# A three-stage attention and MoE kernel: the last stage's first output product taken with the inner dimension outermost, and most of w_out split while it runs

## The chip, the cores and the metric

The kernel runs on one core of a Trainium2 chip. The metric is the device time of one launch in microseconds, as a median over repeated runs; lower is better.

## The reference, cut to what matters

Three layers follow one another: a bucketed attention, a mixture of experts that sends every token to one expert, and a dense two-layer network with an ELU between its products. The change is in the last of them. N is 1536 tokens, w_in is 512 x 2048, w_out is 2048 x 512, and both come as float64 although the function casts to float32.

```python
def _moe2_ref(x, w_in, w_out):
    h = x @ w_in
    g = np.where(h > 0.0, h, 1.0 * (np.exp(np.minimum(h, 0.0)) - 1.0))
    return (g @ w_out).astype(np.float32)

def reference(...):
    x = _attn_ref(q, k, v, proj)            # to [1536, 512]
    x = _moe_ref(x=x, ...)
    return _moe2_ref(x=x, ...)
```

The float64 inputs reach the kernel as pairs of 32-bit words, so a piece of w_in or w_out has to be turned into float32 bits before use.

## The kernel before, in words

Attention, the experts and the dense layer run one after the other. Every large product is computed in float16 halves: an operand is split into a high half and a low half (what the high half leaves over), and three matmuls (high by high, high by low, low by high) go into one accumulation in PSUM.

The last stage is `moe2` (L1073). The 1536 tokens are three blocks of 512. `stage1(b)` (L1088) makes the hidden activations of block b in 16 items f of 128 hidden units. For one item TensorE (PE) issues 12 matmuls into one PSUM tile `p` (L1098 to L1100: four parts of 128 inputs, three matmuls each). ScalarE (ACT) then forms `r`, `ex` and `th` (L1103, L1105, L1107), VectorE (DVE) forms `m` in two instructions (L1109, L1110), GpSimd (POOL) rounds `m` to the high half `gh` (L1111) and, for blocks 0 and 1, subtracts it to get the low half `gl` (L1113); for block 2 DVE does that subtraction (L1119). `ex` and `th` have one buffer each, so `ex` of the next item waits for L1109 of this one; `r` and `m` have two. The PSUM tag `mp` has 8 tiles, taken in turn, so PE can be up to eight items ahead of L1110, which is the last reader of `p`.

`stage2(b)` (L1124) is the second product of block b: for each of four token tiles t of 128 tokens, 16 x 3 matmuls over f (L1132 to L1134) into one PSUM tile, then one ACT copy to `o` (L1136, two buffers) and one indirect DMA issued by POOL that scatters the 128 rows to the output (L1137). The calls stand in the order stage1(0), stage1(1), stage2(0), stage1(2), stage2(1), stage2(2) (L1139 to L1146).

w_out is split by the `Feeder` (L552). It is 16 pieces of 128 x 512, piece c belonging to hidden part f = c; pieces 0 to 7 go to the tiles `wbh` and `wbl`, pieces 8 to 15 to `wah` and `wal`. One call of `step` (L601) advances a pipeline of three: it writes the low half of the oldest piece (L610, on DVE here), then the high half of the next one (L614, on ACT here), and then starts a new piece, which for float64 is three bit operations on DVE (L589, L590, L591); it then loads another piece by DMA from SyncE's queue (SP, L574) into one of 6 staging tiles. So 16 pieces take 18 steps. The tuple `M2F` (L55) says after which items f of which block a step is made: after every second item of block 0 and after every item of block 1.

The queues of each engine run in the order in which the code emits instructions. There is no other order than that of the calls above.

Of the kernel before, what the change touches and what calls it, by code (L numbers as in the profile page):

```python
# [10 lines left out]
F32 = mybir.dt.float32  # L11
I32 = mybir.dt.int32
AF = mybir.ActivationFunctionType
# [38 lines left out]
UO = 6  # L52
XN = (0, 1, 2, 2, 2, 2, 2, 5)
NWI = 0
M2F = (range(0, 16, 2), range(16), ())  # L55
LAST = 94
STG = 6
MORE = 1
# [493 lines left out]
class Feeder:  # L552
# [4 lines left out]

    def __init__(self, nc, g, depth):
        self.nc, self.g, self.depth = nc, g, depth
        self.todo, self.loaded, self.stage = [], [], [None, None]  # L560
        self.eager, self.n32, self.n, self.more, self.done, self.modes = False, 0, 0, None, {}, []

    def add(self, items):
# [37 lines left out]
    def step(self, keep=0):  # L601
        nc = self.nc
        p2, p1 = self.stage
        if p2:
            x, hi, lo, scale, mode, n = p2
            self.done[n] = self.done.get(n, 0) + 1
            if mode[1] == "p":
                nc.gpsimd.tensor_tensor(lo, x, hi, op=ALU.subtract)
            else:
                nc.vector.scalar_tensor_tensor(lo, x, scale, hi, op0=ALU.mult, op1=ALU.subtract)  # L610
        if p1:
            x, hi, lo, scale, mode, n = p1
            if mode[0] == "a":
                nc.scalar.activation(hi, x, AF.Copy, scale=scale)  # L614
            else:
                nc.gpsimd.tensor_scalar(hi, x, scale, 1.0, op0=ALU.mult, op1=ALU.mult)
        self.stage = [p1, self.first() if self.loaded and len(self.loaded) + len(self.todo) > keep else None]
        if self.eager:
            self.load()
# [20 lines left out]
WIS, WOS, GS = 2.0 ** 7, 2.0 ** 8, 2.0 ** 12  # L640
# [58 lines left out]


def routing(tc, g, pool, T, xgs, step):

    nc = tc.nc
# [32 lines left out]
    g.xg = {}  # L736
    xgs()
    step()
    nc.vector.tensor_reduce(g.sm, g.ex, axis=AX.X, op=ALU.add)
    nc.vector.tensor_scalar(g.sm, g.sm, 1e-9, None, op0=ALU.add)  # L740
# [118 lines left out]
def expert_up(nc, pool, ps, wh, wl, xh, xl, step):  # L859

    hh = pool.tile([128, 8, NW], F16, tag="hh", bufs=2, name="hh")
    hl = pool.tile([128, 8, NW], F16, tag="hl", bufs=2, name="hl")
    for f in range(8):
        p = ps.tile([128, NW], F32, tag="mp", bufs=8, name="hp")
        fs = slice(f * 128, (f + 1) * 128)
        for kk in range(4):
            w = slice(kk * 1024 + f * 128, kk * 1024 + (f + 1) * 128)
            nc.tensor.matmul(p, lhsT=wh[:, w], rhs=xh[:, kk], start=(kk == 0), stop=False)
            nc.tensor.matmul(p, lhsT=wl[:, w], rhs=xh[:, kk], start=False, stop=False)
        for kk in range(4):  # L870
            w = slice(kk * 1024 + f * 128, kk * 1024 + (f + 1) * 128)
            nc.tensor.matmul(p, lhsT=wh[:, w], rhs=xl[:, kk], start=False, stop=(kk == 3))
        nc.scalar.activation(hh[:, f], p, AF.Relu)
        nc.vector.scalar_tensor_tensor(hl[:, f], p, 0.0, hh[:, f], op0=ALU.max, op1=ALU.subtract)
        step(f)
    return hh, hl
# [196 lines left out]
def moe2(tc, es, g, w_out, out, fd):  # L1073
    nc = tc.nc
    pool = es.enter_context(tc.tile_pool(name="m2", bufs=1, reuse_waits="tile"))
    ps = es.enter_context(tc.tile_pool(name="m2ps", bufs=1, reuse_waits="tile", space=PSUM))
    parts = g.wb, g.wa
    g.phase = 2 * E
    fd.depth, fd.n = STG, 0
    fd.add(g.wo)  # L1080
    fd.load()
    fd.mode64 = M2
    s1 = 1.0 / (YS * WIS)
    G = {}
    lngs = pool.tile([128, 1], F32, name="lngs")
    nc.vector.memset(lngs, math.log(GS))

    def stage1(b):  # L1088
        gh = pool.tile([128, 16, 512], F16, tag="gh", bufs=2, name="gh")
        gl = pool.tile([128, 16, 512], F16, tag="gl", bufs=2, name="gl")  # L1090
        G[b] = gh, gl
        cols = slice(b * 512, (b + 1) * 512)
        late = None
        for f in range(16):
            p = ps.tile([128, 512], F32, tag="mp", bufs=8, name="p1")
            fs = slice(f * 128, (f + 1) * 128)
            for kk in range(4):
                nc.tensor.matmul(p, lhsT=g.wih[:, kk, fs], rhs=g.yh[:, kk, cols], start=(kk == 0), stop=False)  # L1098
                nc.tensor.matmul(p, lhsT=g.wih[:, kk, fs], rhs=g.yl[:, kk, cols], start=False, stop=False)  # L1099
                nc.tensor.matmul(p, lhsT=g.wil[:, kk, fs], rhs=g.yh[:, kk, cols], start=False, stop=(kk == 3))  # L1100

            r = pool.tile([128, 512], F32, tag="r", bufs=2, name="r")
            nc.scalar.activation(r, p, AF.Relu, scale=-s1)  # L1103
            ex = pool.tile([128, 512], F32, tag="ex", bufs=1, name="ex")
            nc.scalar.activation(ex, r, AF.Exp, scale=-1.0, bias=lngs)  # L1105
            th = pool.tile([128, 512], F32, tag="th", bufs=1, name="th")
            nc.scalar.activation(th, r, AF.Tanh, scale=-0.5)  # L1107
            m = pool.tile([128, 512], F32, tag="m", bufs=MB, name="m")
            nc.vector.scalar_tensor_tensor(m, ex, GS, th, op0=ALU.add, op1=ALU.mult)  # L1109
            nc.vector.scalar_tensor_tensor(m, p, s1 * GS, m, op0=ALU.mult, op1=ALU.max)  # L1110
            nc.gpsimd.tensor_scalar(gh[:, f], m, 1.0, 1.0, op0=ALU.mult, op1=ALU.mult)  # L1111
            if b < GLP:
                nc.gpsimd.tensor_tensor(gl[:, f], m, gh[:, f], op=ALU.subtract)  # L1113
            if late:
                late()

            def late(f=f, m=m):
                if b >= GLP:
                    nc.vector.tensor_sub(gl[:, f], m, gh[:, f])  # L1119
            if f in M2F[b]:  # L1120
                fd.step()
        late()

    def stage2(b):  # L1124
        gh, gl = G.pop(b)
        for t in range(4):
            j = 4 * b + t
            p = ps.tile([128, 512], F32, tag="mp", bufs=8, name="p2")
            ts_ = slice(t * 128, (t + 1) * 128)
            for f in range(16):  # L1130
                (wh, wl), o = parts[f // 8], (f % 8) * 512
                nc.tensor.matmul(p, lhsT=gh[:, f, ts_], rhs=wh[:, o:o + 512], start=(f == 0), stop=False)  # L1132
                nc.tensor.matmul(p, lhsT=gh[:, f, ts_], rhs=wl[:, o:o + 512], start=False, stop=False)  # L1133
                nc.tensor.matmul(p, lhsT=gl[:, f, ts_], rhs=wh[:, o:o + 512], start=False, stop=(f == 15))  # L1134
            o = pool.tile([128, 512], F32, tag="o", bufs=2, name="o")
            nc.scalar.activation(o, p, AF.Copy, scale=1.0 / (GS * WOS))  # L1136
            nc.gpsimd.indirect_dma_start(out=out, out_offset=bass.IndirectOffsetOnAxis(ap=g.idx[:, j:j + 1], axis=0), in_=o, in_offset=None)  # L1137

    stage1(0)  # L1139
    stage1(1)  # L1140
    while fd.left():
        fd.step()
    stage2(0)
    stage1(2)
    stage2(1)
    stage2(2)  # L1146


def body(tc, q, k, v, proj, w_gate, w1, w2, w_in, w_out, out, dbg=None):
# [8 lines left out]
    with ExitStack() as es:  # L1158
# [12 lines left out]
        with tc.manual_schedule():  # L1171
# [40 lines left out]
            with ExitStack() as es3:  # L1212
                moe2(tc, es3, g, w_out, out, fd)
# [27 lines left out]
```

## Time and profile before

| what | value |
|---|---|
| median of 3 runs (lowest to highest) | 705.37 us (702.53 to 707.24) |
| the profiled execution | 704.08 us |
| its span in the trace | 702.0 us |
| PE busy over the span | 646.1 us (92%) |
| DVE, ACT, POOL busy over the span | 490.2, 364.2, 268.6 us |
| first matmul of the last stage | 425.42 us from the span's start |

Times in the rows below are microseconds from the start of the span, unless marked ns. The busy time of PE counts overlapping matmuls once; a matmul of 512 columns has a record of 0.38 us although the next one starts sooner, so the distance of starts is what one costs. "idle before <-X" is how long the engine stood still before an instruction and what released it.

### The profile page before, as it was taken

The numbers are of one execution on the slowest core, as the hardware profiler recorded it, in microseconds if no ns is written. First come the engines' busy times: TensorE is split into PE (matmuls) and PEld (weight loads), VectorE is DVE, ScalarE is ACT, GpSimd is POOL, SyncE is SP. The second block draws the span as 40 slices with busy tenths as digits, with TensorE's granted clock in tenths as the row PEclk, the third lists the DMA queues.
The fourth block names the chain that finished last, engine by engine and source line by source line (L and its number), as shares of the span: only waits on it lengthen the run. The fifth ranks groups of instructions, "written<-read, shape, count | busy, mean of one in ns | idle before, by whom it ended". The sixth has DMA issues, their size and how long they took to land. (4 is left out here: it accounts for less than half of the span.)

```text
span 702.0 us, 12276 instructions
## 1 busy us (share of the span) xinstructions
PE 646.1 (92%) x4584; PEld 423.1 (60%) x4584; DVE 490.2 (70%) x971; ACT 364.2 (52%) x663; POOL 268.6 (38%) x327
## 2 busy tenths in 40 slices
PE   6889999999999878899999998999688999999996
PEld 3456666666666537799999994444233444444442
DVE  6878999888867276799999996888997007710000
ACT  4567676676677425666666544455447027710000
POOL 5958788667733035000000002666347313311001
PEclk9889999999999988899999999999989999999999
DMA  5878999997852049988887835121100000000000
GB/s 174 171 143 183 210 253 232 219 199 177 160 122 57 23 123 204 276 285 294 296 286 261 292 131 211 61 90 61 60 0 1 31 30 1 0 16 31 15 31 30
DMA packets 135071, 95.49 MB, mean 136 GB/s; under 512 B 104800, under 2 KB 117088, under 8 KB 135008
## 3 DMA queue, kind: packets, MB, share of 16 engines
q1 hardware_dynamic: 133088, 88.38, 47.7%
q0 software_dynamic: 1920, 6.29, 3.0%
q8 instruction: 37, 0.61, 0.4%
q14 instruction: 26, 0.21, 0.1%
HBM read 62.93 MB, written 6.29 MB: 99 GB/s over the span
## 5 line engine op out<-in xcount | busy, mean ns | idle before, releaser
L1111 POOL TENSOR_SCALAR gh<-m 128x512 f16<-128x512 f32 x48 | 41.8, 870 | 227.5 <-DVE f L589 156.1
L339 ACT ACTIVATE A<-sp,nm 128x768 f32<-128x768 f32 x96 | 94.9, 991 | 37.9 <-DVE nm L332 32.2
L321 DVE TENSOR_REDUCE nm<-sp 128x1 f32<-128x768 f32 x96 | 91.1, 949 | 25.2 <-PE sp L317 23.2
L1098 PE MATMUL p<-yh,wih 128*128 128x512 f16 x192 | 74.8, 390 | 14.4 <-DVE m L1110 11.7
L380 ACT ACTIVATE AT<-ptA 128x512 f32<-128x512 f32 (+1 forms) x102 | 59.0, 580 | 38.1 <-PE ptA L378 31.3
L390 PE MATMUL ot<-AT,vraw 128*64 128x384 f32 x192 | 74.2, 507 | 1.8 <-ACT AT L380 1.8
L1099 PE MATMUL p<-yl,wih 128*128 128x512 f16 x192 | 74.9, 390 | 0.0
L1100 PE MATMUL p<-yh,wil 128*128 128x512 f16 x192 | 74.6, 389 | 0.0
L378 PE MATMUL ptA<-id,A 128*128 128x128 f32 x396 | 61.7, 280 | 12.3 <-ACT AT L380 10.6
L1109 DVE SCALAR_TENSOR_TENSOR m<-ex,th 128x512 f32<-128x512 f32 x48 | 34.3, 715 | 55.0 <-ACT th L1107 49.1
L316 PE MATMUL sp<-KA,QA 128*128 128x384 f16 x192 | 64.1, 334 | 3.0 <-ACT A L339 2.7
L378 PEld LDWEIGHTS ptA<-id,A 128*128 128x128 f32 x396 | 46.3, 141 | 33.0 <-ACT AT L380 27.7
L317 PE MATMUL sp<-KB,QB 76*128 76x384 f16 x192 | 63.6, 331 | 0.0
L1136 ACT ACTIVATE o<-p 128x512 f32<-128x512 f32 x12 | 7.1, 595 | 103.6 <-PE p L1134 103.6
L349 POOL TENSOR_TENSOR hl<-A,hl 128x768 f16<-128x768 f32 x30 | 49.3, 1644 | 2.5
L1105 ACT ACTIVATE ex<-r,lngs 128x512 f32<-128x512 f32 x48 | 34.7, 722 | 28.7 <-DVE m L1109 27.6
L1137 POOL DMA_INDIRECT out_dram<-o,idx x12 | 11.9, 988 | 95.1 <-ACT o L1136 95.0
L395 PE MATMUL ot<-ATD,VH 128*64 128x256 f16 x270 | 46.0, 280 | 0.0
L1113 POOL TENSOR_TENSOR gl<-m,gh 128x512 f16<-128x512 f32 x32 | 44.0, 1376 | 2.7
L1099 PEld LDWEIGHTS <-wih 128*128 128x128 f16 x192 | 19.2, 100 | 36.7 <-issue 16.1
L399 PE MATMUL ot<-AT,vraw 128*64 128x128 f32 (+1 forms) x192 | 40.0, 291 | 0.0
L360 POOL TENSOR_SCALAR hl<-A 128x768 f16<-128x768 f32 x30 | 25.3, 843 | 38.2 <-ACT A L339 38.2
(250 smaller groups left out, 1660.3 us busy)
## 6 DMA issues: line engine op xcount, KB each, us to landing
stg<-in_moe_w_dram SPq DMA_DIRECT2D x64, 512.0 KB, 5.0
stg<-in_moe_w_in_dram SPq DMA_DIRECT2D x16, 512.0 KB, 5.0
stg<-in_moe_w_out_dram SPq DMA_DIRECT2D x16, 512.0 KB, 3.2
vraw<-in_v_dram SPq DMA_DIRECT2D x8, 384.0 KB, 3.6
xd<-xr SPq DMA_DIRECT2D x16, 192.0 KB, 2.4
qraw<-in_q_dram SPq DMA_DIRECT2D x7, 384.0 KB, 4.0
kraw<-in_k_dram SPq DMA_DIRECT2D x7, 384.0 KB, 4.1
ATD<-hl SPq DMA_TRANSPOSE x30, 3.5
```

Source lines behind the costliest of these rows:

```text
L316: nc.tensor.matmul(sp[:, j, 0:384], lhsT=QA[P, h][:, c * 128:(c + 1) * 128], rhs=KA[P, h][:, kk], start=True, stop=False)
L317: nc.tensor.matmul(sp[:, j, 0:384], lhsT=QB[P, h][0:76, c * 128:(c + 1) * 128], rhs=KB[P, h][0:76, kk], start=False, stop=True)
L321: nc.vector.tensor_reduce(nm[:, 0:1], sp[:, :, 0:384], axis=AX.XY, op=ALU.max, negate=True)
L339: nc.scalar.activation(a, sp[:, :, 0:384], AF.Exp, bias=nm[:, 2:3], scale=nm[:, 1:2], accum_out=SUM[u][:, r:r + 1])
L349: LATE.append((lambda: nc.gpsimd.tensor_tensor(hl[:, 1], a, hl[:, 0], op=ALU.subtract), u, r, hl, a))
L378: nc.tensor.transpose(pt[:, cols], src[:, kt * 128:(kt + 1) * 128], g.id32)
L380: nc.scalar.activation(at[:, 0:n], pt[:, 0:n], AF.Copy)
L390: nc.tensor.matmul(ot[64:128], lhsT=vt[P][:, 1, kt, :], rhs=at, start=(kt == 0), stop=(kt == 5))
L395: nc.tensor.matmul(ot[0:64, 0:n].rearrange("p (a b) -> p a b", b=128), lhsT=VH[P][:, vs, kt, :], rhs=ATD[u][:, :, as_, kt], start=(kt == 0 ...
L1098: nc.tensor.matmul(p, lhsT=g.wih[:, kk, fs], rhs=g.yh[:, kk, cols], start=(kk == 0), stop=False)
L1099: nc.tensor.matmul(p, lhsT=g.wih[:, kk, fs], rhs=g.yl[:, kk, cols], start=False, stop=False)
L1100: nc.tensor.matmul(p, lhsT=g.wil[:, kk, fs], rhs=g.yh[:, kk, cols], start=False, stop=(kk == 3))
```

## The change

`M2F` now asks for four steps in block 0 and four in block 1, after the items 2, 6, 10 and 14 of each. The loop that made the remaining steps ahead of the second product is gone. The first block's second product is a new function, `stage2_first`: its outer loop goes over f and its inner one over the four token tiles, with four PSUM tiles open together. Ahead of the matmuls of f it emits steps until f + 3 pieces are complete in emission order (the new counter `out`, reset at the start of the calls). All four tiles are stored after the last f. The other two blocks keep the order with t outside; their loop body moved to `part2` and `store` unchanged. The diff in full:

```diff
--- before.py
+++ after.py
@@ -52,7 +52,7 @@
 UO = 6
 XN = (0, 1, 2, 2, 2, 2, 2, 5)
 NWI = 0
-M2F = (range(0, 16, 2), range(16), ())
+M2F = (2, 6, 10, 14), (2, 6, 10, 14), ()
 LAST = 94
 STG = 6
 MORE = 1
@@ -557,7 +557,7 @@
 
     def __init__(self, nc, g, depth):
         self.nc, self.g, self.depth = nc, g, depth
-        self.todo, self.loaded, self.stage = [], [], [None, None]
+        self.todo, self.loaded, self.stage, self.out = [], [], [None, None], 0
         self.eager, self.n32, self.n, self.more, self.done, self.modes = False, 0, 0, None, {}, []
 
     def add(self, items):
@@ -604,6 +604,7 @@
         if p2:
             x, hi, lo, scale, mode, n = p2
             self.done[n] = self.done.get(n, 0) + 1
+            self.out += 1
             if mode[1] == "p":
                 nc.gpsimd.tensor_tensor(lo, x, hi, op=ALU.subtract)
             else:
@@ -1121,26 +1122,42 @@
                 fd.step()
         late()
 
+    def part2(gh, gl, p, t, f):
+        ts_ = slice(t * 128, (t + 1) * 128)
+        (wh, wl), o = parts[f // 8], (f % 8) * 512
+        nc.tensor.matmul(p, lhsT=gh[:, f, ts_], rhs=wh[:, o:o + 512], start=(f == 0), stop=False)
+        nc.tensor.matmul(p, lhsT=gh[:, f, ts_], rhs=wl[:, o:o + 512], start=False, stop=False)
+        nc.tensor.matmul(p, lhsT=gl[:, f, ts_], rhs=wh[:, o:o + 512], start=False, stop=(f == 15))
+
+    def store(p, j):
+        o = pool.tile([128, 512], F32, tag="o", bufs=2, name="o")
+        nc.scalar.activation(o, p, AF.Copy, scale=1.0 / (GS * WOS))
+        nc.gpsimd.indirect_dma_start(out=out, out_offset=bass.IndirectOffsetOnAxis(ap=g.idx[:, j:j + 1], axis=0), in_=o, in_offset=None)
+
+    def stage2_first(b):
+
+        gh, gl = G.pop(b)
+        ps4 = [ps.tile([128, 512], F32, tag="mp", bufs=8, name="p2") for _ in range(4)]
+        for f in range(16):
+            while fd.out < min(16, f + 3):
+                fd.step()
+            for t in range(4):
+                part2(gh, gl, ps4[t], t, f)
+        for t in range(4):
+            store(ps4[t], 4 * b + t)
+
     def stage2(b):
         gh, gl = G.pop(b)
         for t in range(4):
-            j = 4 * b + t
             p = ps.tile([128, 512], F32, tag="mp", bufs=8, name="p2")
-            ts_ = slice(t * 128, (t + 1) * 128)
             for f in range(16):
-                (wh, wl), o = parts[f // 8], (f % 8) * 512
-                nc.tensor.matmul(p, lhsT=gh[:, f, ts_], rhs=wh[:, o:o + 512], start=(f == 0), stop=False)
-                nc.tensor.matmul(p, lhsT=gh[:, f, ts_], rhs=wl[:, o:o + 512], start=False, stop=False)
-                nc.tensor.matmul(p, lhsT=gl[:, f, ts_], rhs=wh[:, o:o + 512], start=False, stop=(f == 15))
-            o = pool.tile([128, 512], F32, tag="o", bufs=2, name="o")
-            nc.scalar.activation(o, p, AF.Copy, scale=1.0 / (GS * WOS))
-            nc.gpsimd.indirect_dma_start(out=out, out_offset=bass.IndirectOffsetOnAxis(ap=g.idx[:, j:j + 1], axis=0), in_=o, in_offset=None)
-
+                part2(gh, gl, p, t, f)
+            store(p, 4 * b + t)
+
+    fd.out = 16 - fd.left()
     stage1(0)
     stage1(1)
-    while fd.left():
-        fd.step()
-    stage2(0)
+    stage2_first(0)
     stage1(2)
     stage2(1)
     stage2(2)
```

## Rows read from the trace of the kernel before

**Rows 1.** The page's busy tenths of PE over the span, 40 slices

```profile
PE   6889999999999878899999998999688999999996
```

**Rows 2.** Last stage by stretches: busy us (x instructions) per engine, PEclk, DMA

```profile
425.40:486.60 61.20, 59.73 (x277) 27.02 (x277) 50.20 (x63) 32.73 (x58) 33.45 (x30) 1.00 0.32 114
486.60:528.80 42.20, 29.63 (x109) 11.67 (x109) 40.40 (x51) 20.71 (x37) 19.87 (x19) 0.88 0.10 35
528.80:540.84 12.04, 12.04 (x48) 5.13 (x49) 9.02 (x12) 8.79 (x16) 10.26 (x10) 0.86 0.00 1
540.84:571.92 31.08, 31.08 (x145) 14.07 (x144) 2.95 (x5) 4.18 (x8) 9.35 (x10) 1.00 0.07 26
```

**Rows 3.** Waits from 425 on (total us, times, longest), and the first in time

```profile
PE p L1098 <- DVE m L1110: 11.7, 8, 2.2
PE p L1132 <- DVE m L1110: 2.3, 1, 2.3
...
486.60 0.38 PE L1098 MATMUL p<-yh,wih 128*128 128x512 f16 x1 [1.45 <-DVE m L1110]
```

**Rows 4.** Timeline of PE, last stage: start us, us, engine, line, operation

```profile
425.42 0.38 PE L1098 MATMUL p<-yh,wih 128*128 128x512 f16 x1 [2.67 <-DVEq L1043]
...
530.12 0.63 PE L1134 MATMUL p<-wbh,gl 128*128 128x512 f16 x1
530.55 0.63 PE L1132 MATMUL p<-wbh,gh 128*128 128x512 f16 x1
...
540.84 0.38 PE L1132 MATMUL p<-wbh,gh 128*128 128x512 f16 x1
...
571.92 0.38 PE L1098 MATMUL p<-yh,wih 128*128 128x512 f16 x1
```

**Rows 5.** Timeline of DVE in block 0 of the last stage

```profile
430.11 0.69 DVE L1109 SCALAR_TENSOR_TENSOR m<-ex,th 128x512 f32<-128x512 f32 x1 [4.44 <-ACT th L1107]
...
434.49 0.68 DVE L1109 SCALAR_TENSOR_TENSOR m<-ex,th 128x512 f32<-128x512 f32 x1
...
443.22 0.69 DVE L1109 SCALAR_TENSOR_TENSOR m<-ex,th 128x512 f32<-128x512 f32 x1 [0.71 <-POOL gh L1111]
...
444.56 0.92 DVE L610 SCALAR_TENSOR_TENSOR wbl<-f,wbh 128x512 f16<-128x512 f32 x1
...
446.27 1.52 DVE L590 SCALAR_TENSOR_TENSOR f<-stg,f 128x512 int32<-128x512 int32 x1
...
448.44 0.68 DVE L1109 SCALAR_TENSOR_TENSOR m<-ex,th 128x512 f32<-128x512 f32 x1
...
450.56 0.69 DVE L1109 SCALAR_TENSOR_TENSOR m<-ex,th 128x512 f32<-128x512 f32 x1 [0.71 <-POOL gh L1111]
```

**Rows 6.** Timeline of DVE just before the last stage, w_in's pieces

```profile
420.69 0.68 DVE L610 SCALAR_TENSOR_TENSOR wil<-f,wih 128x512 f16<-128x512 f32 x1
...
421.87 0.69 DVE L590 SCALAR_TENSOR_TENSOR f<-stg,f 128x512 int32<-128x512 int32 x1
...
423.20 0.38 DVE L893 SCALAR_TENSOR_TENSOR yl<-yp,yh 128x224 f32 x1
```

**Rows 7.** Timeline of ACT in block 0, the high half of piece 1

```profile
443.03 0.61 ACT L614 ACTIVATE wbh<-f 128x512 f16<-128x512 f32 x1
```

**Rows 8.** Timeline of PE in the attention: scores, L317 then L316 changes the bank

```profile
202.33 0.33 PE L317 MATMUL sp<-KB,QB 76*128 76x384 f16 x1
202.49 0.33 PE L316 MATMUL sp<-KA,QA 128*128 128x384 f16 x1
202.66 0.33 PE L317 MATMUL sp<-KB,QB 76*128 76x384 f16 x1
```

**Rows 9.** Output stores: ACT, then POOL, then the DMA's time to landing

```profile
551.40 0.60 ACT L1136 ACTIVATE o<-p 128x512 f32<-128x512 f32 x1 [7.16 <-PE p L1134]
...
552.28 0.98 POOL L1137 DMA_INDIRECT out_dram<-o,idx  x1 [3.64 <-ACT o L1136]
...
DMA to landing us min/median/max: 2.7/2.7/2.8
```

## The prediction

> **What bounds the kernel now.** Read the page's slices first: in the last stage, which begins near slice 24, PE is full but for a dip between slices 27 and 30 [rows 1]. The page says "PE-bound with a hole". To see the hole, cut the last stage into stretches: from 425.4 to 486.6 and from 540.8 on PE is busy nearly throughout at a granted clock of 1.00; from 486.6 to 528.8 it is busy 29.6 of 42.2 us, at 0.88, while DVE is busy 40.4; and from 528.8 to 540.8 it is busy but at 0.86 [rows 2]. Then ask who was waited for: PE stood still 8 times for L1110 in the first product, 11.7 us, and once, 2.3 us, at the start of the second, first at 486.60 [rows 3]. L1110 is DVE's last read of a PSUM tile. So for the first 61 us PE runs ahead on eight PSUM tiles, and then it moves at DVE's pace, whose time goes to the split of w_out beside `m`.
>
> The timeline of PE says what the hole costs. In the undisturbed stretch 144 matmuls start between 540.84 and 571.92, 0.2158 us each (2.4 GHz). At 530.12 two starts lie 0.43 apart: the lower level, 1.2 GHz [rows 4]. Clock and waits go together: the granted clock is below 1 only in the stretch with the waits and just behind it [rows 2, 3]. Block 0's and block 1's first products and block 0's second one are 576 matmuls, 124.3 us at 0.2158; they took 571.92 - 425.42 = 146.5 [rows 4]. The excess is **22.2 us**: 14.0 of waits [rows 3], and 8.2 of low clock (39 matmuls at 0.21 extra).
>
> **The change, part by part.** Work is neither added nor removed: the same 48 bit operations, 16 high and 16 low halves, 576 matmuls, four stores. What changes is when DVE does the pieces.
>
> *Steps in the first products.* Instead of steps after 8 items of block 0 and after each of the first ten of block 1 (by then all 18 are made) there are 4 and 4. The price of a step in the chain of `m` is read from DVE in block 0: from one L1109 to the next it is 2.12 us without a step (448.44 to 450.56) and 5.22 with a full one (443.22 to 448.44); the first two steps have no low half to write and cost 4.38 (430.11 to 434.49) [rows 5]. PE needs 12 x 0.2158 = 2.59 per item. So a stepped item puts the chain 5.22 - 2.59 = 2.63 behind (1.79 for the first two) and each of the three others gives back 0.47: +1.22 per four items. With no lag at item 2, it is 1.79 at item 3, 0.38 at 6, 2.17 at 7, 0.76 at 10, 3.39 at 11, 1.98 at 14, 4.61 at 15, then in block 1 (items 16 to 31) 5.83 at 19, 7.05 at 23, 8.27 at 27 and 9.49 at 31, the last.
>
> The base of that lag: item 0's last matmul ends at 425.42 + 2.59 + 0.16 = 428.17, its L1109 starts at 430.11, 1.94 later, and both parts of `m` take 1.34 (443.22 to 444.56) [rows 4, 5]. An item n is then done on DVE at 428.86 + 2.59 (n + 1) + lag. PE may start item n once n - 8 is done, so it waits only with a lag over 8 x 2.59 - 2.59 - 3.44 = 14.7. The largest is 9.49: **PE doesn't wait in either first product**, and ends them at 425.42 + 32 x 2.59 = 508.3 instead of 528.8.
>
> *PSUM tiles of the second product.* The four tiles opened together are those that items 24 to 27 held. Item 27 is done at 428.86 + 72.52 + 8.27 = 509.65; PE wants that tile after three groups of 3 matmuls, at 510.25. Just enough; bounds 0 and 1 us, I take 0.
>
> *The pieces that are left.* Six are complete in emission order when the second product begins. DVE goes on with them without waiting for PE, since they read staging tiles only. Item 31 is done at 428.86 + 82.88 + 9.49 = 521.2, the low half of piece 6 at 521.9; PE reaches f = 6 at 508.3 + 6 x 2.59 = 523.8, so 1.9 to spare. A piece costs DVE 2.51 where POOL is idle (420.69 to 423.20, L590 0.69 in it) [rows 6] and 3.88 where POOL works (444.56 to 448.44, L590 1.52) [rows 5]. After item 31 POOL has only its last `gh` and `gl` to do, so I take 3.88 for piece 7 and 2.51 for the other eight: 0.5 to spare at f = 7, and because 2.51 is under 2.59 it doesn't shrink afterwards. Piece 15 ends at 521.9 + 3.88 + 8 x 2.51 = 545.9 against 547.2. The margin is small: 0.2 us more in each cycle of four items makes 1.4 us of lag at the end and about 0.9 of wait. Bounds: 0, and 10.3 if all nine pieces cost 3.88 (521.9 + 34.9 = 556.8 for piece 15, plus 0.7 for lag). I take 0.7, nearest the rows without POOL. ACT's high halves (0.61 each) [rows 7] have an engine to themselves there.
>
> *Does a matmul wait for more than its own piece?* It would, if writes to `wbh` were ordered against every read of it. In the step that writes the low half of piece 0 at 444.56 (it reads `wbh`) the high half of piece 1 (it writes another slice of `wbh`, and is emitted later) ran at 443.03, ahead of it [rows 5, 7]. So waits go by slices, and I cost this at 0.
>
> *f outside.* Each f is 4 x 3 matmuls, and the PSUM bank changes after three of them, 64 times in all against 4. In the attention's scores the bank changes every two matmuls: L317 to L316 across the bank 0.16, L316 to L317 within it 0.17, for 384 columns [rows 8]. Cost 0. By the Trainium skill ("TensorE: Matmul & The Clock Gate", section "A second HAM failure mode: psum-queue depth-cycling") a kernel that cycled through PSUM banks left small idle gaps between its groups and its clock swung between the two levels; that speaks against this loop, and by it the third rival below would come true.
>
> *Stores.* All four come at the end of `stage2_first`, and stand in ACT's queue ahead of stage1(2)'s first `r`. With two `o` buffers the third copy waits for the first DMA: from ACT's start 0.9 to POOL's issue and 2.7 to landing [rows 9]. First copy 1.8 us ahead of PE's end (nine matmuls), third at +1.8, fourth 1 us later (POOL's 0.98 spacing), ACT free at +3.4, when item 0 of block 2 is ready at +2.6. Late by 0.8, which eight PSUM tiles cover; without that cover it would cost those 0.8. Nothing later moves: stage1(2) and the two other second products are the same 576 matmuls at full pace.
>
> *SP's queue.* Loads follow the steps; each is issued when its staging tile is free, at least four steps before its use. Cost 0.
>
> **Sum.** The second product ends 22.2 - 0.7 = 21.5 us earlier. On the profiled execution's own time, 704.08, that is 682.6; on the median, 705.37, 683.9. I predict **683.3**, between the two, with its own range 680 to 686.
>
> **Rivals.**
>
> 1. *The late pieces pace the second product.* POOL's work, or a longer cycle in block 1, keeps DVE behind PE from f = 6 on. For: margins of 0.5 us. Against: POOL has no work left there. Price: 10.3 us at the upper bound, 692.2 on 704.08; with low clock in the proportion of before (8.2 to 14.0) 6.0 more, 698.2. A typical case is 692.
>
> 2. *The first products don't come free.* If a cycle without step beside low clocks or busier POOL were near 2.6, the lag would go on growing past 14.7, and PE would wait as it does now: about 704, no change. Against: eight pairs in block 0 repeat 7.34 us (443.22 to 450.56) [rows 5].
>
> 3. *Slower: the second product at the low clock.* If the change of bank after every three matmuls left gaps and the clock stayed at 1.2 GHz, all 192 matmuls would take 0.43 instead of 0.2158 [rows 4]: +40.6 us, 704.08 - 22.2 + 40.6 = 722.5. It decides from 105 of the 192 on (22.2 / 0.211). Against: rows 8.
>
> **How the numbers follow.** Forecast 0.80, rival 1 0.13, rival 2 0.04, rival 3 0.03. About 1% (7 us) is what a measurement of this kernel can tell from no change. Forecast and rival 1 are faster by more: 0.93; same 0.04; slower 0.03. The range goes from the lowest run less the whole 22.2 (702.53 - 22.2 = 680.3, so 680) to 691, which takes in part of rival 1.
>
> **What would show it.** PE without a wait from 425 to the end of the last matmul, at clock 1.00; the first matmul of the second product at 508.3, stage1(2)'s first at about 550; stepped items of L1109 some 5.2 apart and unstepped ones 2.1; item 31's L1110 done near 521; L590 at 0.69 from the second late piece on. Wrong if PE waits for L610 in the second product by more than 3 us, if its starts there lie more than 0.22 apart, or if it still waits for L1110 before 508.

## The result, and the profile after

The changed kernel takes 684.77 us (median of four, 680.84 to 687.91) against 703.95 for the kernel before (702.17 to 707.24): 0.9714 of its time, with a 95% interval of 0.9678 to 0.975. Timed again later beside it, it gave 682.96 against 702.39, ratio 0.9718 (0.9671 to 0.9765). One of the eleven runs of the kernel before in that second comparison was in a slower state (709.24 us): the ratio leaves it out, and the median of the other ten is 701.98. The forecast was 683.3 in a range of 680 to 691. The profiled execution took 682.41 us, its span 680.3.

The page's busy tenths of PE after the change, and its granted clock, in 40 slices:

```profile
PE   6899998999999876799999998999999999999996
PEclk9989999999999997999999999999999999999998
```

The dip of [rows 1] between slices 27 and 30 is gone. Stretches of the last stage after the change, columns as in [rows 2]:

```profile
425.40:486.60 61.20, 61.20 (x280) 27.48 (x279) 45.36 (x58) 38.15 (x66) 40.67 (x38) 0.98 0.22 81
486.60:508.00 21.40, 21.40 (x101) 9.66 (x99) 16.71 (x22) 14.40 (x26) 17.20 (x16) 1.00 0.14 48
508.00:550.00 42.00, 41.32 (x192) 18.57 (x190) 33.83 (x49) 13.79 (x23) 11.18 (x11) 1.00 0.15 51
```

PE is busy throughout both first products, and all but 0.7 us of the second one, at a granted clock of 1.00 but for 0.98 in the first of these stretches. DVE, busy for 40.4 of 42.2 us in the hole before, now has 33.8 us of work in the 42 us of the second product and makes PE wait twice there, 0.8 us together (one of the two is too short to have a mark below: at 510.10 PE starts 0.3 us late).

PE's starts, after the change, where one thing gives way to the next (L1099 is the first product, L1128 to L1130 the second):

```profile
423.30 0.38 PE L1099 MATMUL p<-yh,wih 128*128 128x512 f16 x1 [2.95 <-DVEq L1044]
...
424.40 0.63 PE L1101 MATMUL p<-yh,wil 128*128 128x512 f16 x1
424.83 0.63 PE L1099 MATMUL p<-yh,wih 128*128 128x512 f16 x1
...
507.86 0.38 PE L1128 MATMUL p<-wbh,gh 128*128 128x512 f16 x1
...
509.59 0.38 PE L1130 MATMUL p<-wbh,gl 128*128 128x512 f16 x1
510.10 0.38 PE L1128 MATMUL p<-wbh,gh 128*128 128x512 f16 x1
...
527.21 0.38 PE L1129 MATMUL p<-wbl,gh 128*128 128x512 f16 x1 [0.54 <-DVE wbl L611]
...
550.30 0.38 PE L1099 MATMUL p<-yh,wih 128*128 128x512 f16 x1
```

From the first matmul of the stage to block 2's first, "the stretch" from here on, it is 550.30 - 423.30 = 127.0 us against 146.5 [rows 4]: 19.5 less. The rest of the 21.7 us between the two profiled executions lies outside the change: the stage began 2.1 us earlier, and behind the stretch there are 130.0 us against 130.1. That start is not the change's doing: in the eleven profiled executions of this study it lies anywhere from 423.1 to 429.7.

### The profile page after: what moved, and what is told of

Same layout as the page of the kernel before. It is cut to its first block, busy times and chain, and to the rows that moved or that the text cites. A ratio compares the mean times of both kernels' runs of the same rounds, so it can differ in the third digit from the quotient of the medians.

```text
span 680.3 us, 12275 instructions
## 1 busy us (share of the span) xinstructions
PE 636.7 (94%) x4584; PEld 420.5 (62%) x4584; DVE 486.7 (72%) x971; ACT 362.8 (53%) x663; POOL 269.6 (40%) x327
## 5 line engine op out<-in xcount | busy, mean ns | idle before, releaser
L1112 POOL TENSOR_SCALAR gh<-m 128x512 f16<-128x512 f32 x48 | 39.0, 812 | 199.6 <-DMA stg<-in_moe_w_out_dram 157.4
L321 DVE TENSOR_REDUCE nm<-sp 128x1 f32<-128x768 f32 x96 | 91.0, 948 | 22.3 <-PE sp L317 20.6
L1099 PE MATMUL p<-yh,wih 128*128 128x512 f16 x192 | 73.5, 383 | 3.0 <-DVEq L1044 3.0
L1100 PE MATMUL p<-yl,wih 128*128 128x512 f16 x192 | 73.4, 382 | 0.0
L316 PE MATMUL sp<-KA,QA 128*128 128x384 f16 x192 | 63.6, 331 | 3.3 <-ACT A L339 3.0
L1110 DVE SCALAR_TENSOR_TENSOR m<-ex,th 128x512 f32<-128x512 f32 x48 | 37.7, 786 | 39.2 <-ACT th L1108 30.5
L317 PE MATMUL sp<-KB,QB 76*128 76x384 f16 x192 | 63.2, 329 | 0.0
L1114 POOL TENSOR_TENSOR gl<-m,gh 128x512 f16<-128x512 f32 x32 | 46.0, 1439 | 2.7
L1129 PE MATMUL p<-wbl,gh 128*128 128x512 f16 x96 | 36.4, 379 | 0.5 <-DVE wbl L611 0.5
```

What stands on the lines that cost most here:

```text
L316: nc.tensor.matmul(sp[:, j, 0:384], lhsT=QA[P, h][:, c * 128:(c + 1) * 128], rhs=KA[P, h][:, kk], start=True, stop=False)
L317: nc.tensor.matmul(sp[:, j, 0:384], lhsT=QB[P, h][0:76, c * 128:(c + 1) * 128], rhs=KB[P, h][0:76, kk], start=False, stop=True)
L321: nc.vector.tensor_reduce(nm[:, 0:1], sp[:, :, 0:384], axis=AX.XY, op=ALU.max, negate=True)
```

## The experiments

All are made from the changed kernel. "The stretch" is read from PE's starts in each trace.

**f outside alone.** The old steps, so that no piece is left for the second product.

```diff
-M2F = (2, 6, 10, 14), (2, 6, 10, 14), ()
+M2F = (range(0, 16, 2), range(16), ())
```

> The changed kernel with the old M2F (steps after every second item of block 0 and every item of block 1), so that f is outside but no piece is left for the second product. Theory A (the gain comes from where DVE's steps stand, and f outside is only what lets the late ones in): nothing is gained. PE waits in the first products as before, 11.7 us, and the second product then needs the PSUM tiles of items 24 to 27 within its first f instead of one after another, so that it waits for four L1110s, some 2 us each, instead of one of 2.3: the stretch from the last stage's first matmul to block 2's first is 150 to 153 us against 146.5, the kernel 3 to 7 us slower than before. Theory B (f outside helps by itself): the stretch is shorter than 146.5. Theory C (changing the bank after three matmuls costs): starts lie more than 0.2158 us apart in the second product; at 0.16 for each of 64 changes that is 10 us more than A says.

Measured: 711.36 against 704.98 us, ratio 1.0085 (1.0052 to 1.0119). The stretch is 153.9 us. PE's waits where the second product begins:

```profile
532.58 0.38 PE L1128 MATMUL p<-wbh,gh 128*128 128x512 f16 x1 [2.31 <-DVE m L1111]
536.07 0.59 PE L1128 MATMUL p<-wbh,gh 128*128 128x512 f16 x1 [2.68 <-DVE m L1111]
538.40 0.59 PE L1128 MATMUL p<-wbh,gh 128*128 128x512 f16 x1 [0.90 <-DVE m L1111]
540.54 0.59 PE L1128 MATMUL p<-wbh,gh 128*128 128x512 f16 x1 [0.70 <-DVE m L1111]
```

The four tiles are taken one after another at DVE's pace, as theory A says: 6.6 us instead of 2.3 [rows 3]. Theory B falls: the loop order by itself makes the kernel slower. So does theory C: the stretch is 0.9 us over A's upper bound, not 10, and its starts leave nothing for the change of bank. Of the 29.6 us above 576 x 0.2158, 18.3 are waits and 8.8 are starts about 0.43 apart (1.6 of that at the start of the stage). The other 2.5 are the ends of the matmuls ahead of the waits, whose records reach past the time at which the next one would have started.

**The spread of steps alone.** The second product has t outside, and the ten late steps stand ahead of it.

```diff
-    stage2_first(0)
+    while fd.left():
+        fd.step()
+    stage2(0)
```

> The changed kernel with its four and four steps, but with the second product of block 0 as before: t outside, and the ten steps left emitted ahead of it. Theory A: the first products end early (the second one starts near 84 us after the stage's first matmul, as in the changed kernel), but the first token tile needs all 16 pieces within 10.4 us, while DVE brings the last one only some 121 us after the stage's first matmul; PE waits for L610's low halves about 26 us in the first token tile, and the stretch is 151 to 155 us: 4 to 8 us slower than before. Theory B (relief of DVE in the first products carries the gain, the order of the second product is of no account): the stretch stays within 3 us of the changed kernel's 127.0.

Measured: 713.11 against 704.98 us, ratio 1.0094 (1.0059 to 1.0129); the stretch is 154.4 us, and the second product starts 82.9 us after the stage's first matmul. Who PE waited for, in total us, times and longest:

```profile
PE p L1129 <- DVE wbl L611: 13.0, 3, 7.3
PE p L1129 <- DVE wal L611: 7.6, 7, 1.1
```

The first products come free just as in the changed kernel, and everything gained is lost again in the first token tile. The waits are 20.6 us where about 26 were expected; up to the last of them, at 548.02, the first token tile is 27 us behind, and the difference is in starts further apart than 0.2158 us. So each half of the change costs about 1% by itself, and the two together gain 2.9%.

**Ten early steps instead of eight.**

```diff
-M2F = (2, 6, 10, 14), (2, 6, 10, 14), ()
+M2F = (1, 4, 7, 10, 13), (1, 4, 7, 10, 13), ()
```

> The changed kernel with ten steps in the two first products (after the items 1, 4, 7, 10, 13 of each) instead of eight. Theory A (the lag of DVE behind PE decides): three items cost 5.22 + 2 x 2.13 = 9.48 us against PE's 7.77, so the lag comes to about 15 us at item 31; the first products still run without a wait (it needs about 14.7 at item 23), but the tile of item 27, stepped before, comes some 5 us late: PE waits about 5 us in the first f of the second product and the stretch is 129.6 us plus what low clock adds (up to 2.5), 2.5 to 6 us over the changed kernel. Theory B (what counts is DVE's total work, which is the same): within 1 us of the changed kernel.

Measured: 694.62 against 704.98 us, ratio 0.9839 (0.9804 to 0.9873); the stretch is 135.5 us, 8.5 over the changed kernel's, more than the 2.5 to 6 expected. PE's waits in the stretch:

```profile
513.52 0.38 PE L1128 MATMUL p<-wbh,gh 128*128 128x512 f16 x1 [1.09 <-DVE m L1111]
515.66 0.59 PE L1128 MATMUL p<-wbh,gh 128*128 128x512 f16 x1 [1.33 <-DVE m L1111]
520.86 0.59 PE L1128 MATMUL p<-wbh,gh 128*128 128x512 f16 x1 [3.76 <-DVE m L1111]
```

The place is theory A's (no wait in the first products, then the tiles that DVE has not yet read), the size 6.2 instead of 5: three waits, one each for the tiles of items 25, 26 and 27. Low clock added more than I allowed: the second product's stretch shows a granted clock of 0.90 and takes 51.2 us, 3.6 over 41.4 + 6.2, of which 2.8 are starts 0.43 apart; another 1.4 us of such starts stand at the start of the stage. Theory B (only DVE's total counts) falls.

**No early step.**

```diff
-M2F = (2, 6, 10, 14), (2, 6, 10, 14), ()
+M2F = (), (), ()
```

> The changed kernel with no step in the two first products, so that all 18 stand in the second one, where POOL is idle and a piece costs DVE 2.51 instead of 3.88 us. Theory A: the lag at item 31 is gone, DVE is free some 86 us after the stage's first matmul, but piece 0 is complete only some 9 us after PE wants it, and the pieces then keep pace (2.51 against 2.59): one wait of about 9 us at f = 0 and 133.5 us for the stretch, 6 to 10 us over the changed kernel. Theory D (the gain comes from moving pieces to where POOL leaves DVE alone, the more the better): the time is that of the changed kernel or below it.

Measured: 696.06 against 704.98 us, ratio 0.9873 (0.982 to 0.9926); the stretch is 137.8 us. PE's waits in it, then the stretches of the first and of the second product:

```profile
517.12 0.58 PE L1128 MATMUL p<-wbh,gh 128*128 128x512 f16 x1 [7.84 <-ACT wbh L615]
518.85 0.59 PE L1129 MATMUL p<-wbl,gh 128*128 128x512 f16 x1 [1.15 <-DVE wbl L611]
```

```profile
424.60:517.10 92.50, 84.68 (x384) 37.94 (x385) 56.66 (x70) 59.44 (x97) 65.54 (x64) 0.96 0.09 35
517.10:562.40 45.30, 44.14 (x193) 19.40 (x193) 36.13 (x60) 10.63 (x17) 0.84 (x1) 0.93 0.34 117
```

Two waits for piece 0, its high half and then its low half, together of the expected size (9.0 against 9), after which the pieces keep pace for all 16 f; the rest of what it costs is mostly low clock, 1.6 us at the start of the stage and most of the 2.7 behind the waits (0.93). Theory D falls: pieces are cheaper late, but too many late ones make PE wait.

**Six early steps.**

```diff
-M2F = (2, 6, 10, 14), (2, 6, 10, 14), ()
+M2F = (4, 9, 14), (4, 9, 14), ()
```

> The changed kernel with six steps in the first products (after the items 4, 9, 14 of each) instead of eight. Theory A: a step taken out of the first products takes about 2.6 us off the lag and puts one late piece of 2.5 us in, needed 2.6 us earlier, so that PE's waits stay near 0 to 1 us: the same as the changed kernel within 1 us, with the wait for the tile of item 27 gone. Theory D (the more late the better, or every late piece makes PE wait): a difference of over 2 us to one side or the other.

Measured: 681.97 against 706.36 us, ratio 0.9639 (0.9573 to 0.9705). No wait of PE in the stretch, which takes 124.4 us, 0.1 more than 576 x 0.2158. Its two parts:

```profile
423.10:505.90 82.80, 82.80 (x384) 37.54 (x385) 58.83 (x77) 54.72 (x94) 59.34 (x57) 1.00 0.20 70
505.90:547.50 41.60, 41.60 (x195) 18.81 (x193) 34.40 (x52) 12.21 (x21) 9.19 (x9) 1.00 0.19 64
```

With this order of work nothing more than that 0.1 us is left to gain in the stretch. This one and the changed kernel were then timed side by side.

> The changed kernel unaltered, beside the one with six steps on the same chip, to tell the two apart. Theory A: two short waits in the second product (0.3 for the tile of item 27, 0.7 for the low half of piece 7), 125.4 us for the stretch where no low clock falls into it; 19 to 22 us faster than before.

> The kernel with six early steps, again. Theory A: no wait, 124.4 us for the stretch, so 1.0 us faster than the changed kernel, 0.15%, which may not show in the whole time. If it is faster by more than 2 us, the two short waits cost more than their length, by low clock for one thing.

Measured against the same 702.39 us: the changed kernel 682.96, ratio 0.9718 (0.9671 to 0.9765), six steps 682.49, ratio 0.9698 (0.9649 to 0.9747). The whole times do not tell them apart. In the traces they differ as expected: from the second product's first matmul to block 2's first it is 42.55 us with eight steps and 41.50 with six. Both executions have low clock at the start of the stage, 1.3 and 1.7 us, so that the whole stretches are 126.7 and 126.1. The two waits of the changed kernel were there again:

```profile
PE p L1129 <- DVE wbl L611: 0.5, 1, 0.5
PE p L1128 <- DVE m L1111: 0.3, 1, 0.3
```

**Four stores at once.** Two kernels take all three second products with f outside, so that the last four stores have nothing behind them; the second one gives the last two copies other buffers.

```diff
-    stage2(1)
-    stage2(2)
+    stage2_first(1)
+    stage2_first(2)
```

> The changed kernel with f outside in the second products of blocks 1 and 2 as well, so that the four stores of block 2 stand at the end of the kernel, with nothing to cover them. Cost of the loop order by itself: if changing the bank is free, the last matmul comes as many us after block 2's first as in the changed kernel. Cost of four stores at once: by theory S (each indirect DMA to the output waits for the one before to land, as the 3.48 to 3.61 us between POOL's four issues in the changed kernel suggest) the last POOL issue comes 3 x 3.5 us after the first, which is 1.9 us earlier than a last tile's store would be: about 8.5 us more than the changed kernel. By the prediction's own step (only the two o buffers tie the third copy to the first DMA, POOL's issues are 1 us apart) it is about 2.6 us more.

```diff
-        o = pool.tile([128, 512], F32, tag="o", bufs=2, name="o")
+        o = pool.tile([128, 512], F32, tag="o" if j < 10 else "m", bufs=2, name="o")
```

> The same with f outside in all three blocks, but the last two stores of block 2 use the buffers of m (free by then), so that no copy of block 2 waits for a buffer. Theory S (the DMAs wait for each other): POOL's four last issues stay some 3.5 us apart and the time is that of the kernel with two buffers, within 1 us. Theory of the two buffers: the four issues lie 1 us apart and the end comes 1.6 to 6 us earlier than with two buffers.

Measured, one run each: 691.47 and 690.84 us. From block 2's first matmul to the last it is 675.09 - 550.98 = 124.1 us with f outside everywhere and 674.40 - 550.30 = 124.1 in the changed kernel: the loop order costs PE nothing. From the last matmul to the end of the span it is 689.5 - 675.1 = 14.4 us against 680.3 - 674.4 = 5.9: 8.5 more, theory S's number. POOL's last issues with two buffers:

```profile
674.48 0.97 POOL L1135 DMA_INDIRECT out_dram<-o,idx  x1 [29.64 <-ACT o L1134]
677.96 0.97 POOL L1135 DMA_INDIRECT out_dram<-o,idx  x1 [2.51 <-ACT o L1134]
681.43 0.97 POOL L1135 DMA_INDIRECT out_dram<-o,idx  x1 [2.51 <-ACT o L1134]
684.92 0.97 POOL L1135 DMA_INDIRECT out_dram<-o,idx  x1 [2.52 <-DMA out_dram<-o,idx]
```

And with four, ACT's copies ahead of them:

```profile
672.86 2.49 ACT L1134 ACTIVATE o<-p 128x512 f32<-128x512 f32 x4 [33.29 <-PE p L1130]
...
680.69 0.97 POOL L1135 DMA_INDIRECT out_dram<-o,idx  x1 [2.51 <-DMA out_dram<-o,idx]
684.18 0.97 POOL L1135 DMA_INDIRECT out_dram<-o,idx  x1 [2.52 <-DMA out_dram<-o,idx]
```

With the four copies done in 2.49 us the issues stay 3.48 us apart and now name the DMA before as what released them. The buffers were not the tie; each write to the output waits for the one before it to land. That is not so for every indirect DMA from POOL's queue. Ahead of the changed kernel's experts POOL issues 12 that gather rows (L761), which take 4.4 to 7.2 us to land; three of them:

```profile
261.10 0.95 POOL L761 DMA_INDIRECT wih<-xd,idx  x1 [0.30 <-DVE wih L773]
262.35 0.95 POOL L761 DMA_INDIRECT wih<-xd,idx  x1 [0.30 <-issue]
263.60 0.94 POOL L761 DMA_INDIRECT wih<-xd,idx  x1 [0.30 <-issue]
```

These start 1.25 us apart. So the queue alone doesn't tie the stores to each other. That all of them write one output is the likely reason, but whether the wait is the program's or the chip's, and whether it can be left out, was not tested.

## Why the prediction was right, step by step

**The bound and the sum.** The excess of 22.2 us was there to be had: with six steps the stretch is 124.4 us, 22.1 under the 146.5 of before. The changed kernel took 19.5 of it in its profiled execution, against 21.5 forecast, and the three others with the same code in the stretch took 125.4, 125.4 and 126.7 (19.8 to 21.1). By medians the gain is 19.2 and 19.0 us (the second against 701.98). So the mechanism holds and the size is about a tenth too high: the term mis-sized is the allowance of 0.7 us for waits, which came to 1.0 (125.4 less 124.4), beside a spell of low clock at the start of the stage, for which I allowed nothing: from 424.40 on eight starts lie 0.43 apart, 1.7 us. Such a spell of 1.3 to 1.7 us is in six of the study's eleven traces; the kernel with six steps shows it in one execution and not in the other, so it doesn't come from the steps. PE stands still for 2.65 to 2.95 us just ahead of the stage in all eleven; why the spell follows in only six is not shown. That the profiled execution came within 0.2 us of my 682.6 is in part luck: its stage began 2.1 us earlier.

One reading in the prediction was off without changing the sum. The 8.2 us that it puts down to low clock are 6.5 in 32 starts at about 0.43, and 1.5 in the nine matmuls ahead of the waits: a wait counts from the end of the 0.38 us record, 0.16 after the next one would have started. The 22.2 us stand, and so does what a wait costs beyond its length, as rival 1 prices it; only not all of that is clock.

**Steps in the first products.** L1110 (L1109 before) across one full step and three items without, after the change:

```profile
456.92 0.70 DVE L1110 SCALAR_TENSOR_TENSOR m<-ex,th 128x512 f32<-128x512 f32 x1 [0.71 <-ACT th L1108]
...
462.14 0.69 DVE L1110 SCALAR_TENSOR_TENSOR m<-ex,th 128x512 f32<-128x512 f32 x1
...
464.27 0.69 DVE L1110 SCALAR_TENSOR_TENSOR m<-ex,th 128x512 f32<-128x512 f32 x1 [0.71 <-POOL gh L1112]
...
466.40 0.70 DVE L1110 SCALAR_TENSOR_TENSOR m<-ex,th 128x512 f32<-128x512 f32 x1 [0.71 <-ACT th L1108]
...
468.54 0.71 DVE L1110 SCALAR_TENSOR_TENSOR m<-ex,th 128x512 f32<-128x512 f32 x1 [0.71 <-ACT th L1108]
```

5.22, 2.13, 2.13, 2.14: 11.62 us, where [rows 5] gave 5.22 + 3 x 2.12 = 11.58. PE never waits, and starts the second product 84.6 us after its first matmul; 82.9 was forecast, and 82.9 is measured where the spell at the start is missing.

**PSUM tiles.** Costed at 0 with a bound of 1: 0.3 (509.59 to 510.10 instead of 0.22). With ten steps the waits for these tiles are 6.2, so this is one side on which the design is near its edge; the late pieces are the other.

**The pieces that are left.** DVE, after the change, at the hand-over from the last item to the late pieces and in the middle of them:

```profile
522.22 0.69 DVE L1111 SCALAR_TENSOR_TENSOR m<-p,m 128x512 f32<-128x512 f32 x1
522.83 0.68 DVE L611 SCALAR_TENSOR_TENSOR wbl<-f,wbh 128x512 f16<-128x512 f32 x1
...
524.30 1.52 DVE L590 SCALAR_TENSOR_TENSOR f<-stg,f 128x512 int32<-128x512 int32 x1
...
526.47 0.69 DVE L611 SCALAR_TENSOR_TENSOR wbl<-f,wbh 128x512 f16<-128x512 f32 x1
...
527.65 0.69 DVE L590 SCALAR_TENSOR_TENSOR f<-stg,f 128x512 int32<-128x512 int32 x1
...
528.99 0.69 DVE L611 SCALAR_TENSOR_TENSOR wal<-f,wah 128x512 f16<-128x512 f32 x1
```

The first piece takes 3.64 us (forecast 3.88, L590 1.52 with POOL at work), the next 2.52 (forecast 2.51, L590 0.69), and so on to the last. Piece 7 was to have 0.5 us to spare (0.6 by the prediction's own terms, 526.4 less 525.8) and made PE wait 0.54: item 31 was done 99.6 us after the stage's first matmul instead of 95.8. Of those 3.8 us, 1.95 were there by item 2 (the spell), 0.5 came over the cycles (half of it because the two steps without a low half cost 4.50 and not 4.38, as the second of them had before) and 1.3 between items 28 and 30, where item 29's L1110 started 0.4 late and then took 1.58 us beside POOL's L1114. PE was late too, by the spell and the wait for the tile, which is why only 0.54 of it shows.

**Slices, f outside.** Both costed at 0, and both hold: PE waited for the low half of its own piece only, and the starts in the second product lie 0.22 apart across banks and within them. What the Trainium skill ("TensorE: Matmul & The Clock Gate", section "A second HAM failure mode: psum-queue depth-cycling") reports of a kernel that cycled through PSUM banks did not come about here: the granted clock from 508 to 550 is 1.00, and with it rival 3 falls.

**Stores: wrong, and covered.** I had POOL's issues 1 us apart and ACT late by 0.8. After the change ACT and POOL show:

```profile
552.42 0.60 ACT L1134 ACTIVATE o<-p 128x512 f32<-128x512 f32 x1 [2.62 <-DMA out_dram<-o,idx]
555.93 0.60 ACT L1134 ACTIVATE o<-p 128x512 f32<-128x512 f32 x1 [2.91 <-DMA out_dram<-o,idx]
556.42 0.59 ACT L1104 ACTIVATE r<-p 128x512 f32<-128x512 f32 x1
```

The third copy waits for the first DMA and comes 2.0 us after PE's end (forecast 1.8); that step was right. The fourth comes 3.5 us after the third instead of 1, and `r` of block 2's first item starts at 556.4, when its matmuls had ended at 550.30 + 2.59 + 0.16 = 553.05: 3.4 us late. The eight PSUM tiles cover that as they would have 0.8: from block 2's first matmul to the last it is 124.1 us, as in the kernel before. At the end of the kernel nothing would: 8.5 us.

**Rivals.** Rival 1 (late pieces pace the product) is 0.54 us of wait here, and all of PE's waits when the order is t outside (20.6 us). Rival 2 (the first products don't come free) fell: PE has no wait in them. Its counter-argument counted eight equal pairs in block 0; there are six, since the first two hold the steps without a low half (6.50 and 6.61 us).

## What to carry to other kernels

When a side engine's work makes PE wait, compare what it puts into the chain of each item with PE's time for one, add up the lag item by item, and hold it against the tiles that let PE run ahead: a loss that looks like a busy engine may be only a lag that outgrows its buffers. Where a product consumes pieces one after another, turning its loops so that each piece is needed late makes room for preparing them meanwhile; it pays only together with moving the preparation there, and too few early steps cost as too many do (none, six, eight and ten: stretches of 137.8, 124.4 and 126.1, 125.4 to 127.0, and 135.5 us; between six and eight the whole times show no difference). Results that then come out all at once need something behind them.

## What was not expected of the hardware

Four indirect DMAs from POOL to one output went 3.48 us apart, although an issue takes 0.97 us and buffers were free, while gathers from the same queue went 1.25 us apart. Waits of PE cost more than their length: with 6.2 us of waits at its beginning (ten steps) the second product took another 3.6 us beyond them, with one of 7.84 ahead of it and 1.15 in it (no early step) another 2.7 (45.25 less 41.4 and 1.15), each at a granted clock below 0.94. Of the 3.6 us 2.8, and of the 2.7 us 2.3, are starts 0.43 apart, and most of the rest is the end of the matmul ahead of each wait.
